# Reordering the first weight block of a delta-rule and two-layer MoE kernel: chunk steps first, four weight pairs early, two loads in flight, grams in units 2 and 4

## The chip, the cores and the metric

The kernel runs on one core of one Trainium2 chip. The time is the device time of one execution in microseconds; lower is better. Times of before are the median of three executions, and one further execution was recorded by the hardware profiler.

## What is computed

A delta-rule recurrence over 768 tokens (4 batches, 8 heads, head size 48), and behind it two feed-forward layers over all 3072 tokens (384 to 2048 to 384).

```python
for t in range(S):
    y[:, :, t] = q_t @ state
    state = state + b_t * outer(k_n_t, v_t - k_n_t @ state)
x = y laid out as (3072, 384)
h = x @ w_in;  g = where(h >= 1, h, where(h <= -1, 0, (h + 1)**2 / 4));  x = g @ w_out
h = x @ w_in2; r = maximum(h, 0);  out = (r * r) @ w_out2
```

## The kernel before

The 768 tokens are cut into 24 chunks of 32. A chunk covers all four batches, so it is 128 rows. Four chunks make a group, and also a block of the first layer. For each group the gram matrices of keys and queries are formed (`gram`, L323), and one triangular system is inverted for the whole group. This inversion, `tri`, starts with a transpose (L423), a few short VectorE steps and the scaling at L453 and L462. Then come 60 alternating GpSimd operations, L483 and L484, in strict sequence, and `end` (L487) is the VectorE transpose that brings the result back. With the inverse, `chunk_steps` carries a chunk through: `ks` and `qs` (L547, subtraction on VectorE at L557), `tr` (L561), `ku` (L596, the state copied back at L603 and L604) and `xt` (L628, split at L630 and L631), which yields the chunk's 128 rows of input for the first layer.

The first layer runs in blocks of four chunks; a block has 16 units, one for each 128 columns of the hidden size. Unit x does the first product into `h` (`hidden`, nine matmuls of 128x512 at L643), the activation (ScalarE L675, VectorE L676, ScalarE L678, VectorE L679), the split of the result in two words (ScalarE L692, VectorE L694), and the second product of unit x - 2 into `acc` (`out_`, nine matmuls at L643; LAG = 2). Every number is kept as a high and a low fp32r word, so each product takes three passes.

A unit has two slots, 2x and 2x + 1. The tables `exa` and `exb`, filled with `put_a` and `put`, say which chunk steps, grams and inversion steps are issued in a slot. In `unit`, slot 2x of `exa` is issued behind the `h` product and the activation.

In block 0 the first layer's weights also have to be made. They arrive as 64-bit numbers (`load_w`, L190, 384 KB each) and are turned into two fp32r words: two passes on ScalarE over the raw bits (L199 and L200, `halves`), the join on VectorE (`make`, L206), the high word on ScalarE (`upper`, L236) and the low word on VectorE (`lower`, L240). Two such loads make a weight pair; pair x holds what the first product of unit x + 1 and the second of unit x - 1 need. Three pairs (READY) are made in the chain of the first four chunks, ahead of unit 0. The others are spread over the units by `between`, which `hidden` calls at four points: behind the first VectorE step, behind the second, behind L692 and behind L694.

All engines take their instructions in the written order in block 0 (`manual_schedule`). The loads stand in SyncE's queue in written order too. `loads(m, ...)` lets m loads be under way: each load waits for the landing of the m-th one ahead of it. A `kqg` load for a gram (two DMAs of 192 KB, L148) takes one of two buffers, so those of chunks 10 and 11 are issued behind the grams of chunks 8 and 9.

The third group's inversion is put from slot `a + 2` on, with `a = max(ready, 13)`, where `ready` is the slot of the group's last grams; its `end` stands in slot 31, and chunk 8, the first that needs it, begins in slot 32.

The first products of block 0 take their PSUM tile from three in turn for units below MANY, and from one ("h") for the others; the two tiles that are then left ("att0", "att1") serve the grams and the chunk steps.

Of the kernel before, what the change touches and what calls it, by code (L numbers as in the profile page):

```python
# [25 lines left out]
def kernel(  # L26
# [41 lines left out]
    KQ, KG = 3, 2  # L68
    WL = 2
    GB = 2  # L70
    MANY = 4

    cst = ctx.enter_context(tc.tile_pool(name="cst", bufs=1))
    wp = ctx.enter_context(tc.tile_pool(name="wp", bufs=1))
# [150 lines left out]
    def halves(x):  # L225
        return sign_bits(raws[x])

    def whole_bits(x):
        for f in halves(x):
            f()  # L230

    def make(x):
        words[x] = joined_words(raws.pop(x), [P, 2, DM])

    def upper(x):
        nc.scalar.copy(weights(x)[:, :, 0], words[x])  # L236

    def lower(x):
        t = weights(x)
        nc.vector.tensor_sub(t[:, :, 1], words.pop(x), t[:, :, 0].bitcast(F32))  # L240
# [543 lines left out]
    SL = 2 * NF  # L784
    SPREAD = 3
    NW, NP = 2 * NF, NF
    READY = 3
    exa, exb = {}, {}
    bits = [f for x in range(READY, NP) for f in (lambda x=x: halves(x)[0](), lambda x=x: halves(x)[1]())]
    bits.reverse()  # L790

    def some(m):
        for _ in range(m):
            if bits:
                bits.pop()()

    def between(f):
        a = READY + f if READY + f < NP else None
        last = a - 1 if f and a is not None else NP - 1 if READY + f == NP else None

        def part(x):
            if x % 2 == 0:
                some(1)
            if x == 0 and last is not None:
                upper(last)
            elif x == 1 and last is not None:
                lower(last)
            elif x == 3 and a is not None:
                make(a)

        return part

    def put(n, slot, *fs):
        for i, f in enumerate(fs):
            exb.setdefault(SL * n + slot + i, []).append(f)
# [9 lines left out]
    def put_a(n, slot, *fs):  # L825
        exa.setdefault(SL * n + slot, []).extend(fs)
# [5 lines left out]
    def run(ex, x):  # L832
        for f in ex.pop(x, ()):
            f()
# [22 lines left out]
    with tc.manual_schedule():  # L857
# [22 lines left out]
        def loads(m, what):  # L880
            flight[0] = m
            for kind, c in what:
                kind(c)
            flight[0] = 0

        def ws(a, z):
            return [(load_w, needed[x]) for x in range(a, z)]

        def kgs(c):
            return [(load_kg, c)]  # L890

        def kvs(c):
            return [(load_kv, c)]

        loads(2, [(load_kg, c) for c in range(4, 8)] + kvs(0) + kvs(1) + ws(0, 4))
        loads(1, kvs(2) + kvs(3) + ws(4, 14))
        begin, pre, steps, end = tri(0, V, True)
        begin()
        pre[0]()
# [44 lines left out]
        s2()  # L944
        q1()
        make(1)
        t2()
        upper(1)
        go(pre1[-2:])
        steps1[0]()  # L950
        go(steps1[1:])
        q2()
        k2()
        lower(1)
        p2()
        y2()
        whole_bits(2)
        s3()
        dld0(3)
        make(2)  # L960
        t3()
        p1()
        x2_()
        upper(2)
        q3()
        p3()
        y3()
        lower(2)
        x1()
        q0()  # L970
        p0()
        x3()
        x0()
        k3()
        loads(2, ws(14, 18) + [(load_kq, 4), (load_kq, 5)] + kgs(8) + kgs(9) + ws(18, 22))
        turn[0] = None

        put(0, 9, lambda: loads(2, ws(22, NW)))
        put(0, 11, end1)
        put(0, 11, lambda: value(4))  # L980
        put(0, 12, lambda: value(5))
# [10 lines left out]
        put(0, SL - 1, lambda: first2(RAW))  # L992

        at, ready = {}, {}
        for c, slot in ((8, 8), (10, 11)):
            ready[c + 1] = slot
            put_a(0, slot, lambda c=c: two_grams(c))
        for n in range(2, NB):
            todo = []
            for j, c in enumerate(range(FIRST[n], FIRST[n] + SIZES[n])):  # L1000
                if n < NB - 1 and 2 * j < SIZES[n + 1]:
                    x = FIRST[n + 1] + 2 * j
# [3 lines left out]
            for i, (mark, s_) in enumerate(todo):  # L1006
                slot = SL * (n - 1) + i * SL // len(todo)
# [16 lines left out]
        for g in range(2, NG):  # L1024
            a, z = ready[GFIRST[g] + GROUPS[g] - 1], at[GFIRST[g]]
            a = max(a, 13)
# [76 lines left out]
```

## Time and profile before

| what | value |
|---|---|
| median of three executions | 1028.0 us (1022.54 to 1029.91) |
| the profiled execution | 1027.41 us |
| its span, first to last instruction | 1025.7 us |
| TensorE (PE) busy | 979.7 us, 96% |
| VectorE (DVE) busy | 518.7 us, 51% |
| ScalarE (ACT) busy | 434.5 us, 42% |
| GpSimd (POOL) busy | 296.5 us, 29% |
| mean granted TensorE clock | 0.992 |

The 1.7 us between the execution and its span lie outside of the program's instructions. Shares are means over the whole span; the stages differ, and the rows below go by stretches.

### The profile page before, as it was taken

The page shows a single profiled execution, that of the slowest core. Times are in us where ns is not written, and L with a number is a line of the kernel's source. Part 1 is how long each engine was busy: PE and PEld are TensorE (multiplying, and loading weights), DVE is VectorE, ACT ScalarE, POOL GpSimd, SP SyncE. Part 2 cuts the span into 40 slices and gives each one's busy share as a digit, 9 for nine tenths or more (in the row PEclk, how much of TensorE's full clock was granted, in tenths as well). Part 3 has the DMA queues.
Part 4 walks back from the last instruction along what each step waited for, and adds up shares of the span by engine and source line. Part 5 has one row for each costly group of instructions (what it writes and reads, how often), then busy time and mean ns, then how long its engine had stood idle before and what let it go on. Part 6 is the DMA issues. An engine that isn't in the chain of part 4 may idle for free.

```text
span 1025.7 us, 29990 instructions
## 1 busy us (share of the span) xinstructions
PE 979.7 (96%) x13416; PEld 832.9 (81%) x13416; DVE 518.7 (51%) x801; ACT 434.5 (42%) x745; POOL 296.5 (29%) x414
## 2 busy tenths in 40 slices
PE   5687888999999999999999999999999999999998
PEld 5676667787888878787888888998999999999997
DVE  4447676565557656655545666543343343333333
ACT  2327456345545534554545554333333333333332
POOL 1479029618605920872201112120020200100000
PEclk9999889999999999999999999999999999999999
DMA  6437741334334432433432223010010000000000
GB/s 128 146 108 218 219 107 48 111 103 141 103 95 133 123 109 84 132 100 109 129 94 86 63 62 124 16 32 31 1 62 1 1 31 1 31 1 1 32 1 31
DMA packets 33937, 80.68 MB, mean 79 GB/s; under 512 B 4368, under 2 KB 11664, under 8 KB 33808
## 3 DMA queue, kind: packets, MB, share of 16 engines
q1 hardware_dynamic: 33808, 78.76, 26.2%
q8 instruction: 105, 1.72, 0.7%
q14 instruction: 24, 0.20, 0.1%
HBM read 63.01 MB, written 15.73 MB: 77 GB/s over the span
## 4 chain that ended last, share of the span: by engine, by line
PE 79%; DMA 10%; POOL 4%; DVE 3%; issue 2%; ACT 1%; SPq 1%; POOLq 0%; ACTq 0%; DVEq 0%
PE h L643 36%; PE acc L643 36%; DMA raw<-in_w_dram 6%; DMA kqt<-in_kq_dram 2%; POOL tx L484 2%; POOL t L483 2%; PE tr L561 1%; PE yy L584 1%; PE sps L596 1%; DMA room<-in_kq_dram 1%; DMA kv<-in_kv_dram 1%; PE yy L547 1%; PE ks L547 1%; DVE gp L487 1%; PE g L323 1%
## 5 line engine op out<-in xcount | busy, mean ns | idle before, releaser
L643 PE MATMUL acc<-w,gg 128*128 128x384 f32 x1152 | 217.1, 337 | 0.2 <-ACT e L702 0.2
L643 PE MATMUL h<-x2s,w 128*128 128x512 f32 x864 | 214.6, 393 | 0.0
L643 PEld LDWEIGHTS acc<-w,gg 128*128 128x128 f32 x1152 | 203.9, 188 | 8.3 <-ACT e L702 0.5
L643 PEld LDWEIGHTS h<-x2s,w 128*128 128x128 f32 x864 | 161.0, 188 | 29.2
L643 PE MATMUL h<-xh,w 128*128 128x512 f32 x576 | 154.1, 404 | 4.4 <-ACT r L675 4.4
L643 PE MATMUL acc<-gh,w 128*128 128x512 f32 x576 | 155.1, 405 | 0.5 <-ACT gh L692 0.5
L683 DVE TENSOR_TENSOR rg<-rg 128x512 f32<-128x512 f32 x96 | 70.0, 729 | 140.7 <-ACT rg L682 140.7
L643 PEld LDWEIGHTS h<-xh,w 128*128 128x128 f32 x576 | 107.0, 191 | 28.5 <-ACT r L675 4.9
L682 ACT ACTIVATE rg<-h,zero 128x512 f32<-128x512 f32 x96 | 66.1, 689 | 138.0 <-PE h L643 138.0
L643 PEld LDWEIGHTS acc<-gh,w 128*128 128x128 f32 x576 | 104.7, 190 | 23.9 <-ACT gh L692 1.0
L694 DVE TENSOR_TENSOR gg<-rg,gg 128x512 fp32r<-128x512 f32 x96 | 67.3, 701 | 104.0 <-ACT gg L692 104.0
L675 ACT ACTIVATE r<-h,one 128x512 f32<-128x512 f32 x96 | 65.9, 686 | 120.6 <-PE h L643 120.2
L692 ACT CAST gg<-rg 128x512 fp32r<-128x512 f32 x96 | 59.7, 622 | 118.8 <-PE acc L643 114.3
L676 DVE TENSOR_SCALAR g<-r 128x512 f32<-128x512 f32 x96 | 47.9, 499 | 109.6 <-ACT r L675 109.2
L484 POOL TENSOR_TENSOR tx<-tx,t 128x30 f32<-128x30 f32 (+9 forms) x150 | 99.5, 664 | 11.4
L694 DVE TENSOR_TENSOR gl<-g,gh 128x512 fp32r<-128x512 f32 x96 | 74.5, 776 | 54.0 <-ACT gh L692 42.6
L483 POOL TENSOR_TENSOR t<-tx,gm 128x30 f32<-128x30 f32 (+9 forms) x150 | 94.5, 630 | 16.6 <-DVE tx L462 5.3
L692 ACT CAST gh<-g 128x512 fp32r<-128x512 f32 x96 | 59.6, 620 | 88.7 <-DVE g L679 72.8
L679 DVE SCALAR_TENSOR_TENSOR g<-r,g 128x512 f32<-128x512 f32 x96 | 76.2, 794 | 36.0 <-ACT g L678 36.0
L643 PE MATMUL h<-xl,w 128*128 128x512 f32 x288 | 82.5, 395 | 0.1
L643 PE MATMUL acc<-gl,w 128*128 128x512 f32 x288 | 82.3, 395 | 0.0
L678 ACT ACTIVATE g<-g 128x512 f32<-128x512 f32 x96 | 60.4, 629 | 31.3 <-DVE g L676 29.8
(119 smaller groups left out, 896.6 us busy)
## 6 DMA issues: line engine op xcount, KB each, us to landing
raw<-in_w_dram SPq DMA_DIRECT2D x64, 384.0 KB, 3.7
kqt<-in_kq_dram SPq DMA_DIRECT2D x82, 192.0 KB, 4.1
kv<-in_kv_dram SPq DMA_DIRECT2D x24, 384.0 KB, 4.0
w2f<-wl SPq DMA_DIRECT2D x32, 192.0 KB, 3.9
w2r<-w2f SPq DMA_DIRECT2D x16, 384.0 KB, 3.0
x<-e SPq DMA_DIRECT2D x18, 256.0 KB, 2.3
x2r<-x SPq DMA_DIRECT2D x6, 768.0 KB, 4.9
out_dram<-e SPq DMA_DIRECT2D x23, 192.0 KB, 2.0
```

The lines of the kernel that those rows point to most:

```text
L483: eng.tensor_mul(t, by.to_broadcast(shape), of.to_broadcast(shape))
L484: return eng.tensor_add(rest, rest, t)
L547: per_bh(lambda b, h, p, pd: nc.tensor.matmul(o[p, h], kqt[c][pd, b // 2, h, x * T:(x + 1) * T], st[pd, b // 2, h], start=h == 0, stop=x = ...
L643: nc.tensor.matmul(o, *((r, l) if swap else (l, r)), **flags)
L675: marks[0] = nc.scalar.activation(r, h, AF.Relu, bias=one)
L676: marks[1] = nc.vector.tensor_scalar(g, r, 2.0, 0.5, ALU.min, ALU.mult)
L678: nc.scalar.activation(g, g, AF.Square)
L679: nc.vector.scalar_tensor_tensor(g, r, -1.0, g, ALU.add, ALU.max)
L682: marks[0] = nc.scalar.activation(r, h, AF.Relu, bias=zero)
L683: marks[1] = nc.vector.tensor_mul(g, r, r)
L692: nc.scalar.copy(ghi, g)
L694: nc.vector.tensor_sub(glo, g, ghi.bitcast(F32))
```

## The change

It does five things. `between` is rewritten: a unit's chunk step or gram from slot 2x is now issued at the first of its four points, ahead of that unit's weight work, and the join of a pair moves from the last point of a unit to the first, its high word from the next unit to the second point of the same unit, and its low word to the second point of the next. READY goes from 3 to 4: a fourth pair, and the raw bits of the fifth, are made in the chain ahead of unit 0. The loads are let two at a time from the weight 10 on, where it was one at a time up to weight 13, and the loads of chunks 8 and 9 for the grams stand behind weight 15. The grams of chunks 8 and 9 move from slot 8 (unit 4) to slot 4 (unit 2), those of 10 and 11 from slot 11 (unit 5) to slot 8 (unit 4), and MANY goes from 4 to 2. The last chunk's state update `k3` moves from ahead of unit 0 into unit 1.

```diff
--- before.py
+++ after.py
@@ -68,7 +68,7 @@
     KQ, KG = 3, 2
     WL = 2
     GB = 2
-    MANY = 4
+    MANY = 2
 
     cst = ctx.enter_context(tc.tile_pool(name="cst", bufs=1))
     wp = ctx.enter_context(tc.tile_pool(name="wp", bufs=1))
@@ -784,9 +784,9 @@
     SL = 2 * NF
     SPREAD = 3
     NW, NP = 2 * NF, NF
-    READY = 3
+    READY = 4
     exa, exb = {}, {}
-    bits = [f for x in range(READY, NP) for f in (lambda x=x: halves(x)[0](), lambda x=x: halves(x)[1]())]
+    bits = [f for x in range(READY + 1, NP) for f in (lambda x=x: halves(x)[0](), lambda x=x: halves(x)[1]())]
     bits.reverse()
 
     def some(m):
@@ -795,18 +795,24 @@
                 bits.pop()()
 
     def between(f):
-        a = READY + f if READY + f < NP else None
-        last = a - 1 if f and a is not None else NP - 1 if READY + f == NP else None
+        def pair(x):
+            return x if READY <= x < NP else None
+
+        word, low = pair(READY + f), pair(READY + f - 1)
 
         def part(x):
-            if x % 2 == 0:
+            if x == 0:
+                run(exa, 2 * f)
                 some(1)
-            if x == 0 and last is not None:
-                upper(last)
-            elif x == 1 and last is not None:
-                lower(last)
-            elif x == 3 and a is not None:
-                make(a)
+                if word is not None:
+                    make(word)
+            elif x == 1:
+                if word is not None:
+                    upper(word)
+                if low is not None:
+                    lower(low)
+            elif x == 2:
+                some(1)
 
         return part
 
@@ -893,7 +899,8 @@
             return [(load_kv, c)]
 
         loads(2, [(load_kg, c) for c in range(4, 8)] + kvs(0) + kvs(1) + ws(0, 4))
-        loads(1, kvs(2) + kvs(3) + ws(4, 14))
+        loads(1, kvs(2) + kvs(3) + ws(4, 10))
+        loads(2, ws(10, 16) + kgs(8) + kgs(9) + ws(16, 20))
         begin, pre, steps, end = tri(0, V, True)
         begin()
         pre[0]()
@@ -944,38 +951,44 @@
         s2()
         q1()
         make(1)
+        upper(1)
+        whole_bits(2)
         t2()
-        upper(1)
         go(pre1[-2:])
         steps1[0]()
         go(steps1[1:])
         q2()
+        lower(1)
+        make(2)
+        upper(2)
         k2()
-        lower(1)
         p2()
+        lower(2)
         y2()
-        whole_bits(2)
+        whole_bits(3)
         s3()
         dld0(3)
-        make(2)
+        make(3)
+        upper(3)
         t3()
         p1()
         x2_()
-        upper(2)
+        lower(3)
         q3()
+        halves(4)[0]()
         p3()
         y3()
-        lower(2)
+        halves(4)[1]()
         x1()
         q0()
         p0()
         x3()
         x0()
-        k3()
-        loads(2, ws(14, 18) + [(load_kq, 4), (load_kq, 5)] + kgs(8) + kgs(9) + ws(18, 22))
+        loads(2, [(load_kq, 4), (load_kq, 5)] + ws(20, 24))
         turn[0] = None
 
-        put(0, 9, lambda: loads(2, ws(22, NW)))
+        put(0, 6, lambda: loads(2, ws(24, NW)))
+        put_a(0, 2, k3)
         put(0, 11, end1)
         put(0, 11, lambda: value(4))
         put(0, 12, lambda: value(5))
@@ -992,7 +1005,7 @@
         put(0, SL - 1, lambda: first2(RAW))
 
         at, ready = {}, {}
-        for c, slot in ((8, 8), (10, 11)):
+        for c, slot in ((8, 4), (10, 8)):
             ready[c + 1] = slot
             put_a(0, slot, lambda c=c: two_grams(c))
         for n in range(2, NB):
```

In SyncE's queue, from the fifth weight load on, before (`raw` are first-layer weights, `kqt` halves of a chunk's keys and queries, `kv` keys and values):

```order
L190 DMA raw<-in_w_dram 128x768 x10
L148 DMA kqt<-in_kq_dram 48x1024 x2
L159 DMA kv<-in_kv_dram 128x768 x3
L190 DMA raw<-in_w_dram 128x768 x4
L148 DMA kqt<-in_kq_dram 48x1024 x8
L190 DMA raw<-in_w_dram 128x768 x4
L148 DMA kqt<-in_kq_dram 48x1024 x4
L190 DMA raw<-in_w_dram 128x768 x10
```

And now:

```order
L190 DMA raw<-in_w_dram 128x768 x12
L148 DMA kqt<-in_kq_dram 48x1024 x4
L190 DMA raw<-in_w_dram 128x768 x4
L148 DMA kqt<-in_kq_dram 48x1024 x2
L159 DMA kv<-in_kv_dram 128x768 x3
L148 DMA kqt<-in_kq_dram 48x1024 x4
L190 DMA raw<-in_w_dram 128x768 x4
L148 DMA kqt<-in_kq_dram 48x1024 x4
L190 DMA raw<-in_w_dram 128x768 x8
```

The loads of chunks 8 and 9 (four halves) now stand ahead of the chain's last loads, and the loads of chunks 10 and 11 (the last four `kqt` ahead of the long row of weights) have two more weight loads ahead of them.

TensorE's order around the grams of chunks 10 and 11 (`g`), before, from unit 5's second product on (`w` with a number is one weight pair):

```order
L643 MATMUL acc_1693<-gh,w_1681 128x512 x2
L643 MATMUL acc_1694<-gh,w_1681 128x512 x2
L643 MATMUL acc_1695<-gh,w_1681 128x512 x2
L643 MATMUL acc_1693<-gl,w_1681 128x512
L643 MATMUL acc_1694<-gl,w_1681 128x512
L643 MATMUL acc_1695<-gl,w_1681 128x512
L323 MATMUL g<-kqt 32x64 x64
L643 MATMUL h<-xh,w_1720 128x512 x6
```

And now, from unit 4's first product on:

```order
L643 MATMUL h<-xh,w_1377 128x512 x6
L643 MATMUL h<-xl,w_1377 128x512 x3
L323 MATMUL g<-kqt 32x64 x64
L643 MATMUL acc_1782<-gh,w_1377 128x512 x2
L643 MATMUL acc_1783<-gh,w_1377 128x512 x2
L643 MATMUL acc_1784<-gh,w_1377 128x512 x2
L643 MATMUL acc_1782<-gl,w_1377 128x512
L643 MATMUL acc_1783<-gl,w_1377 128x512
L643 MATMUL acc_1784<-gl,w_1377 128x512
L643 MATMUL h<-xh,w_1612 128x512 x6
```

Before, these grams stand between unit 5's `acc` and unit 6's `h`. Now they stand behind unit 4's `h`, and three products that were ahead of them are behind them: unit 4's `acc`, unit 5's `h` and unit 5's `acc`.

VectorE around unit 6, the first with a chunk step, before:

```order
L487 STREAM_TRANSPOSE gp<-tx 128x32x32
L676 TENSOR_SCALAR g<-r 128x512
L679 SCALAR_TENSOR_TENSOR g<-r,g 128x512
L240 TENSOR_TENSOR w_1994<-wl,w_1994 128x2x384
L557 TENSOR_TENSOR kv<-kv,ks 128x384
L694 TENSOR_TENSOR gl<-g,gh 128x512
```

And now:

```order
L487 STREAM_TRANSPOSE gp<-tx 128x32x32
L676 TENSOR_SCALAR g<-r 128x512
L557 TENSOR_TENSOR kv<-kv,ks 128x384
L206 SCALAR_TENSOR_TENSOR wl<-raw 128x768
L679 SCALAR_TENSOR_TENSOR g<-r,g 128x512
L240 TENSOR_TENSOR w_1971<-wl,w_1971 128x2x384
L694 TENSOR_TENSOR gl<-g,gh 128x512
```

The subtraction L557 stands directly behind L676 now, and the join L206 stands between L676 and L679, where it stood at the end of the unit.

## Rows read from the trace of the kernel before

**Rows 1.** The page: span, TensorE's busy tenths and its clock in 40 slices.

```profile
span 1025.7 us, 29990 instructions
PE   5687888999999999999999999999999999999998
PEclk9999889999999999999999999999999999999999
```

**Rows 2.** By stretch: length, busy PE, PEld, DVE, ACT, POOL, clock, DMA share, GB/s.

```profile
57.00:99.30 42.30, 34.04 (x812) 27.78 (x813) 20.50 (x28) 23.11 (x37) 37.68 (x61) 0.98 0.56 167
79.30:97.30 18.00, 13.05 (x68) 9.93 (x58) 12.55 (x16) 12.89 (x20) 16.28 (x23) 1.00 0.79 238
97.30:117.80 20.50, 16.72 (x292) 12.99 (x292) 14.63 (x19) 11.89 (x17) 5.26 (x7) 0.83 0.76 199
117.80:145.80 28.00, 23.42 (x525) 18.30 (x526) 18.42 (x29) 16.44 (x26) 0.00 (x0) 0.93 0.66 184
145.80:196.50 50.70, 47.20 (x1096) 37.48 (x1095) 32.98 (x45) 27.36 (x45) 46.16 (x66) 0.94 0.19 57
196.50:400.00 203.50, 201.60 (x4068) 162.51 (x4065) 122.21 (x192) 97.55 (x181) 90.14 (x133) 1.00 0.39 113
```

**Rows 3.** The chain that ended last, 60 to 215 us: start, length, what.

```profile
65.37 3.90 DMA raw<-in_w_dram
...
110.45 5.48 DMA kqt<-in_kq_dram
115.97 1.92 PE g L323 x62
...
145.87 1.28 POOL gm L453
...
193.15 0.13 POOL kv L299
...
196.49 2.23 DVE gp L487
```

**Rows 4.** SyncE's queue in order of time: start, length of the row, loads.

```profile
45.65 34.57 SPq L190 DMA_DIRECT2D raw<-in_w_dram  x10
80.27 0.89 SPq L148 DMA_DIRECT2D kqt<-in_kq_dram  x2
...
101.41 7.19 SPq L190 DMA_DIRECT2D raw<-in_w_dram  x4
108.72 2.04 SPq L148 DMA_DIRECT2D kqt<-in_kq_dram  x4
110.81 17.92 SPq L190 DMA_DIRECT2D raw<-in_w_dram  x10
```

**Rows 5.** TensorE in order of time; in brackets idle time before, and releaser.

```profile
97.30 2.91 PE L643 MATMUL h<-xh,w 128*128 128x512 f32 x6 [4.41 <-ACT r L675]
...
106.59 1.54 PE L643 MATMUL h<-xh,w 128*128 128x512 f32 x6
...
117.83 2.93 PE L643 MATMUL h<-xh,w 128*128 128x512 f32 x6
...
126.63 0.88 PE L561 MATMUL tr<-kv,gp 32*32 32x48 f32 x64 [1.12 <-DVE kv L557]
...
145.68 1.50 PE L561 MATMUL tr<-kv,gp 32*32 32x48 f32 x64 [3.36 <-DVE kv L557]
...
167.08 0.88 PE L561 MATMUL tr<-kv,gp 32*32 32x48 f32 x64 [3.01 <-DVE kv L557]
...
199.31 0.88 PE L547 MATMUL ks<-st,kqt 48*32 48x48 f32 x64 [0.50 <-DVE gp L338]
```

**Rows 6.** ScalarE in order of time: unit 1's and unit 2's first steps, and unit 8's.

```profile
85.94 0.67 ACT L675 ACTIVATE r<-h,one 128x512 f32<-128x512 f32 x1
...
91.13 0.68 ACT L675 ACTIVATE r<-h,one 128x512 f32<-128x512 f32 x1
...
138.48 0.67 ACT L675 ACTIVATE r<-h,one 128x512 f32<-128x512 f32 x1
```

**Rows 7.** VectorE in order of time, units 1 and 8.

```profile
86.17 1.34 DVE L206 SCALAR_TENSOR_TENSOR wl<-raw 128x768 int32<-128x768 int32 x1
...
88.94 0.83 DVE L679 SCALAR_TENSOR_TENSOR g<-r,g 128x512 f32<-128x512 f32 x1 [0.75 <-ACT g L678]
...
143.49 0.96 DVE L206 SCALAR_TENSOR_TENSOR wl<-raw 128x768 int32<-128x768 int32 x1
```

## The prediction, made blind

> **What bounds the kernel now.** I read the page first, then the time by stretch, the chain that ended last, and the engines in order of time where the chain changes engine. The page shows TensorE full from about 200 us on and gaps before it [rows 1]. By stretch, TensorE is busy 201.6 of 203.5 us from 196.5 to 400 us [rows 2], and its work is the same in both kernels. So the change can only move the point at which that full stretch begins. I take the first step of chunk 8, at 199.31 us, as this point [rows 5].
>
> Between 79.3 and 196.5 us the four stretches leave TensorE idle for 4.95, 3.78, 4.58 and 3.50 us, 16.8 in all. The clock of the last three (0.83, 0.93, 0.94) says that another 3.5, 2.0 and 3.0 us are lost at the lower of its two levels, 1.2 in place of 2.4 GHz [rows 2]. That is 25 us on paper.
>
> The chain says why they are not to be had at once. It comes from the weight loads, passes through the load of chunk 11's gram, issued at 110.45 and landed 5.48 us later, and the gram itself at 115.97. Then it goes through block 0 to GpSimd, which starts the third group's inversion at 145.87 and holds the chain until VectorE's transpose at 196.49 [rows 3]. TensorE waits only 0.50 us behind that transpose [rows 5]. So two paths end together: TensorE's own work and GpSimd's 50.6 us of inversion. Whatever makes units 8 to 15 faster on TensorE alone ends in a wait for GpSimd. What counts is when the inversion starts and how long it lasts.
>
> **The loads.** One at a time, ten weights are issued in 34.57 us, 3.8 us for each of nine intervals; two at a time, ten take 17.92 us, 1.95 each [rows 4]. From 80.27 us [rows 4] to the landing at 115.93 there are 18 loads of 384 KB (two halves counted as one): chunk 6, three `kv`, four weights, chunks 4, 5, 8 and 9, four weights, chunks 10 and 11. That makes 1.98 us a load, with one load under way at the start. In the changed kernel pairs begin at weight 10, just behind the issue at 65.37 [rows 3], at 65.7 us, also with one under way. Up to chunk 11's gram there are now 24: six weights, chunks 8 and 9, four weights, chunk 6, three `kv`, chunks 4 and 5, four weights, chunks 10 and 11. So 65.7 + 24 x 1.98 = 113.2; the burst of `kv` loads that no limit holds goes a little faster, and I take 112.5 us. Bounds: at the best stretch's 238 GB/s [rows 2] a load takes 1.65 us, which gives 105.3; at the pace of the four weights from 101.41 (7.19 us for three intervals and an issue of 0.3, 2.29 each [rows 4]), 120.7. So the last gram's load comes about 3.4 us sooner, though two loads at a time save some 12 us, because six more loads stand ahead of it.
>
> **Units 0 to 4.** Before, ScalarE's first steps of units 1 and 2 are 5.19 us apart [rows 6], while a unit is two products of nine matmuls, about 2.06 us each (six in 1.54 [rows 5]). TensorE waits for this ring: 4.41 us ahead of unit 4 [rows 5]. Now the high word leaves the ring, since it runs while VectorE does L679, but the join enters it: 1.34 us between L676 and L679, where VectorE waited 0.75 us [rows 7]. I take 4.7 us a unit, a gain of 0.5. TensorE then reaches the grams of chunks 10 and 11, behind unit 4's first product, at about 100 us, and their data are 10 us away. The gain drowns in this wait. The grams of chunks 8 and 9 in unit 2 are no trouble: their loads are the 7th and 8th, landed at about 84, and TensorE comes there at 86 to 87.
>
> These three edits cost or bring nothing of their own: `k3` (about 0.9 us of TensorE) leaves the front of unit 0 and lies in the ring's slack; the fourth pair's work falls where ScalarE and VectorE are busy 23.1 and 20.5 of 42.3 us [rows 2]; the single `h` tile in units 2 and 3 makes TensorE wait for ScalarE's first step, ahead of the longer wait for the loads. If this cover went, the pair would cost its join and low word, some 2.5 us.
>
> **From the grams to the inversion.** Chunk 11's gram takes 1.9 us [rows 3], to 114.4. Behind it now stand three products that were ahead of it, 6.2 us. After a wait of that length the clock is low for a while: unit 6's product took 2.93 us for six matmuls in place of 1.54 [rows 5]. For the three products together I take 0.9 of loss, between 0 and 2.6. So unit 6 starts at 121.5, which is 3.7 us later than 117.83 [rows 5].
>
> From there GpSimd's start was 28.0 us away. Now unit 6's product is at full clock (1.9 less with its second part). The subtraction stands ahead of the weight work, so `tr`'s wait of 1.12 [rows 5] goes. The join of unit 7 stands earlier, so the inversion's transpose comes about 1.0 sooner. In unit 8 the 7.4 us from ScalarE's step at 138.48 [rows 6] to GpSimd's start lose about 1.6, as the join (0.96 at 143.49 [rows 7]) runs where VectorE used to wait for ScalarE. Together 5.6, so 22.4 are left, and the inversion starts at 143.9, 2.0 us sooner. Its slot is not moved: the first slot is 13 at the least, before and after.
>
> **The inversion and its end.** 50.6 us before. Near its end GpSimd waits for keys and values at 193.15 [rows 3], about 0.9 us in two places; these come with chunk 6's end, which is sooner. One pair's join and low word fewer stand beside it, 2.3 us of VectorE. The second group's steps took 37.7 us of GpSimd beside 20.5 of VectorE, the third's 46.2 beside 33.0 [rows 2]; that is at most 0.68 us for each us, 1.6 for the pair. I take 1.5 less in all, between 0 and 2.5. The transpose then starts at 143.9 + 49.1 = 193.0, which is 3.5 us sooner.
>
> The Trainium skill (SBUF — State Buffer, Who interferes with whom) says that a VectorE instruction with two SBUF inputs and a GpSimd instruction that reads SBUF shut each other out for their whole length. By that rule the pair would be worth its full 2.3 us, the end would be 3.2 less in place of 1.5, and the time 1.7 us lower than below. The rows' slope bears out the direction, and not the full size.
>
> TensorE has about 47 us of work from unit 9's `tr` to chunk 8 (53.6 in the rows, less 3.45 of waits for `tr` and 3.0 of clock), so it is there at 190 to 191 and stands still for some 5 us. What follows may run at the low clock: after idle times of 4.41 and 3.36 us it did, after 3.01 it did not (`tr` at 145.68 took 1.50 us, at 167.08 0.88 [rows 5]). That costs 0 to 3.4 us; I take 1.5. The waits for `tr` of 3.36 and 3.01 us thus go, and come back as one wait ahead of chunk 8.
>
> **Sum.** Inversion's start -2.0, its length -1.5, clock behind the new wait +1.5: -2.0 us. The profiled execution took 1027.41 us, 0.6 below the median of 1028.0, so 1025.4; I give 1025.5.
>
> **The rivals.** First, faster: the loads run at the rate of the best stretch and chunk 11's lands at 105.3. Then the inversion starts 7.2 us sooner still, and the time is 1018. For it: the 238 GB/s; against it: the next stretch had 199 [rows 2], and most of the new loads go in pairs, at 1.95. Chance 0.2, with the case that GpSimd runs the inversion at the second group's pace (some 5 us less, 1020.5).
>
> Second, slower: the loads come later than I have them. VectorE has the masks of chunks 10 and 11 ahead of unit 4's join and activation, so units 4 and 5 stand still with TensorE until the data are there. Each us of the landing is one us of the inversion's start. The break-even is a landing at 114.5, and at the slow pace of 2.29 it is 120.7: 8.2 us on 1025.5, so 1033.7. For it: chunk 11's load now has two more weights ahead of it; against it: the 18 loads before held 1.98. Chance 0.2.
>
> Third, the change doesn't do what it says: the grams stand earlier but the inversion starts when it did, since its slot is the same and unit 8 comes no sooner. Then the saved waits of units 9 and 11 all turn up ahead of chunk 8, and the time is that of before, 1027 to 1028. Chance 0.1.
>
> **How the numbers follow.** My forecast, 1021 to 1029, has 0.5. The range takes in the slower rival up to half of its price and the faster one to its end: 1018 to 1031. One per cent, 10 us, is about what a measurement of this kernel can tell from no change. Faster by more needs the fast loads and the shorter inversion together: 0.13. Slower by more needs loads slower than any row: 0.06. Within 1%: 0.81.
>
> **What the changed profile would show.** Right: TensorE idle for 8 us or more ahead of the second pair of grams, released by a load that lands at 110 to 115; no wait for L557 ahead of units 7 and 11; GpSimd's L453 at 142 to 146; TensorE waiting several us ahead of chunk 8, released behind L487. Wrong: grams that wait for nothing, GpSimd starting before 138, or no wait at chunk 8; then the loads are faster than I have them, or the inversion is not the end.

## The result, and the profile after

The changed kernel takes 1030.99 us (median of 20 executions, 1025.93 to 1035.09). The kernel before, run 20 times, takes 1024.89 (1020.23 to 1029.91); the median of the three shown ahead of the prediction, 1028.0, lay at the upper side of that. The ratio is 1.0053, 95% interval [1.0034, 1.0072]: 5.4 us slower, where some 2 us faster were forecast. Below, kernels of different sets are compared by their ratios to the kernel before of the same set; a difference of 0.001 is 1.02 us. The profiled execution took 1032.13 us, its span is 1030.4.

By stretch, with the columns of [rows 2] (length, busy PE, PEld, DVE, ACT, POOL, clock, DMA share, GB/s), the changed kernel has:

```profile
79.30:97.30 18.00, 15.45 (x244) 11.79 (x243) 14.53 (x17) 13.55 (x20) 16.43 (x21) 1.00 0.80 223
97.30:117.80 20.50, 8.00 (x142) 6.56 (x143) 7.21 (x10) 5.60 (x9) 6.53 (x10) 0.67 0.76 210
117.80:145.80 28.00, 26.82 (x538) 21.22 (x536) 22.13 (x32) 20.92 (x33) 0.00 (x0) 1.00 0.50 133
145.80:196.50 50.70, 46.42 (x1104) 37.02 (x1104) 31.46 (x47) 25.19 (x42) 44.95 (x66) 1.00 0.26 76
196.50:400.00 203.50, 199.14 (x4045) 160.88 (x4046) 121.81 (x191) 96.34 (x179) 89.76 (x133) 0.98 0.38 109
```

TensorE does more than before in the first and third of these, and falls to 8.00 us of 20.50 in the second, at a clock of 0.67. TensorE in order of time shows what that is:

```profile
97.45 1.67 PE L643 MATMUL h<-xh,w 128*128 128x512 f32 x6 [1.72 <-ACT r L675]
98.96 0.85 PE L643 MATMUL h<-xl,w 128*128 128x512 f32 x3
111.84 0.39 PE L323 MATMUL g<-kqt 48*32 48x64 f32 x2 [12.02 <-DMA kqt<-in_kq_dram]
112.55 3.63 PE L323 MATMUL g<-kqt 48*32 48x64 f32 x126 [0.32 <-DMA kqt<-in_kq_dram]
116.11 2.28 PE L643 MATMUL acc<-gh,w 128*128 128x512 f32 x6
...
123.04 1.53 PE L643 MATMUL h<-xh,w 128*128 128x512 f32 x6
...
130.28 0.54 PE L561 MATMUL tr<-kv,gp 32*32 32x48 f32 x32 [0.77 <-issue]
...
146.89 0.88 PE L561 MATMUL tr<-kv,gp 32*32 32x48 f32 x64 [1.50 <-DVE kv L557]
...
192.47 0.85 PE L643 MATMUL acc<-gl,w 128*128 128x512 f32 x3
198.97 1.50 PE L547 MATMUL ks<-st,kqt 48*32 48x48 f32 x64 [5.66 <-DVE gp L338]
```

Unit 4's first product is over at 99.8, and then TensorE stands still for 12.02 us, until the first half of chunk 10's load lands at 111.70; the last of the four halves lands at 113.91. The grams take 3.63 us behind that in place of some 2, at the low clock. Unit 6's product starts at 123.04, 5.2 us later than in [rows 5]. Behind that the rows have two short stops: 0.77 us in the middle of unit 6's `tr`, for which the profile names no releaser, and 1.50 us ahead of unit 9's. Then TensorE is ready for chunk 8 at 193.3 and waits 5.66 us.

VectorE and GpSimd in order of time show the rest of the chain, a wait for the grams and then the inversion's start and end:

```profile
114.53 0.69 DVE L338 TENSOR_TENSOR gp<-g,mask 128x512 f32<-128x512 f32 x1 [11.71 <-PE g L323]
...
196.37 2.02 DVE L487 STREAM_TRANSPOSE gp<-tx 128x1024 f32<-128x1024 f32 x1 [6.00 <-POOL tx L484]
198.22 0.70 DVE L338 TENSOR_TENSOR gp<-g,mask 128x512 f32<-128x512 f32 x1
```

```profile
147.08 1.28 POOL L453 TENSOR_TENSOR gm<-gm,st 128x256 f32<-128x256 f32 x1 [42.79 <-DVE st L442]
```

The row of TensorE's wait names its releaser, and it is not the inverse: chunk 8's first step, `ks`, reads the state and the keys, and writes to the PSUM tile that the grams issued just ahead of it have used. L338, the mask that reads these grams, sets the tile free, and in VectorE's order L338 stands behind L487, which waits for GpSimd. So the inversion holds chunk 8 here by way of VectorE's order; whether L338 ahead of L487 would take the wait away was not tried.

The inversion starts 1.2 us later than in [rows 3] and lasts 49.25 us. Its transpose L487 stands at 196.37 against 196.49, and chunk 8 at 198.97 against 199.31: as far as this point the two kernels end at the same time. The difference of the two spans, 4.7 us, arises behind it, and the experiments have to say how that hangs together with the waits ahead of it.

### The profile page after: what moved, and what is told of

Read it like the earlier page. It is cut to its first block, busy times and chain, and to the rows that moved or that the text cites. A ratio compares the mean times of both kernels' runs of the same rounds, so it can differ in the third digit from the quotient of the medians.

```text
span 1030.4 us, 30002 instructions
## 1 busy us (share of the span) xinstructions
PE 977.3 (95%) x13416; PEld 831.7 (81%) x13416; DVE 518.7 (50%) x801; ACT 435.1 (42%) x745; POOL 297.4 (29%) x414
## 4 chain that ended last, share of the span: by engine, by line
PE 78%; DMA 10%; POOL 4%; DVE 4%; issue 2%; ACT 1%; SPq 1%; ACTq 0%; POOLq 0%; DVEq 0%
PE acc L643 35%; PE h L643 35%; DMA raw<-in_w_dram 5%; DMA kqt<-in_kq_dram 3%; POOL tx L484 2%; POOL t L483 2%; PE tr L561 1%; PE yy L584 1%; PE sps L596 1%; DMA kv<-in_kv_dram 1%; PE yy L547 1%; PE ks L547 1%; DMA room<-in_kq_dram 1%; DVE gm L423 1%; PE g L323 1%
## 5 line engine op out<-in xcount | busy, mean ns | idle before, releaser
L643 PE MATMUL h<-xh,w 128*128 128x512 f32 x576 | 151.9, 399 | 2.8 <-ACT r L675 2.3
L484 POOL TENSOR_TENSOR tx<-tx,t 128x30 f32<-128x30 f32 (+9 forms) x150 | 101.9, 679 | 11.4
L676 DVE TENSOR_SCALAR g<-r 128x512 f32<-128x512 f32 x96 | 48.3, 503 | 109.4 <-ACT r L675 108.8
L483 POOL TENSOR_TENSOR t<-tx,gm 128x30 f32<-128x30 f32 (+9 forms) x150 | 95.2, 635 | 15.2 <-DVE tx L462 4.0
L679 DVE SCALAR_TENSOR_TENSOR g<-r,g 128x512 f32<-128x512 f32 x96 | 77.9, 811 | 22.6 <-ACT g L678 22.6
```

The lines of the kernel that those rows point to most:

```text
L483: eng.tensor_mul(t, by.to_broadcast(shape), of.to_broadcast(shape))
L484: return eng.tensor_add(rest, rest, t)
L643: nc.tensor.matmul(o, *((r, l) if swap else (l, r)), **flags)
L676: marks[1] = nc.vector.tensor_scalar(g, r, 2.0, 0.5, ALU.min, ALU.mult)
L679: nc.vector.scalar_tensor_tensor(g, r, -1.0, g, ALU.add, ALU.max)
```

## The experiments

**Theory A**: the grams of chunks 10 and 11 stand too early for their load; TensorE and all that hangs on it waits, and the third group's inversion, which starts behind them, then holds chunk 8. **Theory B**: the new order of `between` costs the time. **Theory C**: the loss lies behind block 0. The first four kernels each undo or keep one part. The kernel before, run beside them, took 1025.88 us (20 executions).

**The grams of chunks 10 and 11 back in unit 5**, all else changed:

```diff
-        for c, slot in ((8, 4), (10, 8)):
+        for c, slot in ((8, 4), (10, 11)):
```

> The changed kernel with the grams of chunks 10 and 11 put back to slot 11, behind unit 5's second product; all else as changed. Theory A (the place of these grams, ahead of three products and behind two more loads, is the cost): TensorE's wait for them falls from 12.3 to 6 to 8 us, the inversion of the third group starts at 140 to 143 in place of 147.1, its closing transpose at 190 to 192, and the time is 4 to 6 us below the changed kernel, at or just under the kernel before. Theory B (the new order in between, with the join inside VectorE's part of the unit, is the cost): the time stays within 2 us of the changed kernel. Theory C (the time is lost behind block 0, where 3.8 of the 4.7 us between the two profiles appear): as B, within 2 us of the changed kernel, wherever the inversion starts.

1020.41 us, ratio to before 0.9954 [0.9927, 0.9982], by the ratios 10 us below the changed kernel, where Theory A had 4 to 6. The last gram load landed at 108.96, 5 us sooner than in the changed kernel's profile though the queue is the same, TensorE waited 0.17 us for it, and the inversion started at 133.41. So not all of this profile's gain is the slot's. Theories B and C, which had no difference beyond 2 us, do not fit.

**The early place kept, the loads of chunks 10 and 11 put first** (e2 in the expectations below): in the changed kernel the loads of chunks 4 and 5 and four weights stand ahead of them in SyncE's queue; here they stand behind.

```diff
-        loads(2, [(load_kq, 4), (load_kq, 5)] + ws(20, 24))
+        put(0, 4, lambda: loads(2, ws(20, 22) + [(load_kq, 4), (load_kq, 5)] + ws(22, 24)))
```

> The changed kernel with one move in SyncE's queue: the loads of chunks 4 and 5 and of weights 20 to 23 are issued in unit 2, behind the grams of chunks 8 and 9, so that the loads of chunks 10 and 11 stand ahead of them. Theory A: chunk 11's gram data land at 100 to 105 in place of 113.9, TensorE's wait there falls to 5 us or less, the inversion starts at 137 to 140 in place of 147.1, its closing transpose comes at 186 to 189, and the time is 6 to 9 us below the changed kernel, so 1 to 4 below the kernel before. Theory B: no difference to the changed kernel beyond 2 us. Theory C: none beyond 2 us either.

1016.82 us, ratio 0.9910 [0.9886, 0.9934], 15 us below the changed kernel, again more than Theory A's 6 to 9. The last of these loads landed at 99.14. TensorE in order of time, around these grams and around chunk 8:

```profile
97.58 1.65 PE L643 MATMUL h<-xh,w 128*128 128x512 f32 x6 [1.72 <-ACT r L675]
99.07 0.85 PE L643 MATMUL h<-xl,w 128*128 128x512 f32 x3
99.85 1.99 PE L323 MATMUL g<-kqt 48*32 48x64 f32 x128
...
183.95 1.50 PE L547 MATMUL ks<-st,kqt 48*32 48x48 f32 x64 [5.72 <-DVE gp L338]
185.23 1.50 PE L547 MATMUL yy<-st,kqt 48*32 48x48 f32 x64
186.66 2.93 PE L643 MATMUL h<-xh,w 128*128 128x512 f32 x6
```

The same instructions in the same order, with the load there in time: the 12 us of waiting are gone, and the grams take 1.99 us. The wait ahead of chunk 8 is as long as in the changed kernel (5.72), 15 us sooner. From 180.4 us, within that wait, the clock was low for 10.2 us: the product of six took 2.93.

**The new `between` and the fourth pair alone**, with the old loads, gram slots, MANY and `k3`:

```diff
-    READY = 3
+    READY = 4
...
-            if x % 2 == 0:
+            if x == 0:
+                run(exa, 2 * f)
                 some(1)
```

> The kernel before with the new between and four weight pairs in the chain alone; loads, gram slots, MANY and the place of the chunk 3 state update as before. Theory A: this half of the change costs nothing; the grams wait as before or somewhat longer (3 to 5 us), the inversion starts at 141 to 144 in place of 145.9, and the time is 1 to 4 us below the kernel before. Theory B: the time is 4 to 7 us above the kernel before, like the changed kernel. Theory C: within 2 us of the kernel before.

1020.08 us, ratio 0.9941 [0.9922, 0.9961]: 6.0 faster than before, where Theory A had 1 to 4. Theory B falls; this part is a gain. From unit 6's product to the inversion's start it took 23.1 us, where [rows 5] and [rows 3] have 28.0. Unit 6's `tr` waits for nothing here, and chunk 8 waits as long as in the changed kernel:

```profile
122.95 0.88 PE L561 MATMUL tr<-kv,gp 32*32 32x48 f32 x64
123.76 1.66 PE L643 MATMUL h<-xh,w 128*128 128x512 f32 x6
...
192.14 1.50 PE L547 MATMUL ks<-st,kqt 48*32 48x48 f32 x64 [5.69 <-DVE gp L338]
```

So the wait of 5.7 us ahead of chunk 8 comes with the new order and the inversion's unmoved slot, not with the late grams: it is 5.66 to 5.72 us in all six profiles that have both, whether the kernel gains or loses, and the 6.0 us of gain are what is left with this wait in.

**The loads, the gram slots and MANY alone**, with the old `between` and three pairs:

```diff
-    MANY = 4
+    MANY = 2
...
-        for c, slot in ((8, 8), (10, 11)):
+        for c, slot in ((8, 4), (10, 8)):
```

> The kernel before with the new loads, gram slots and MANY of 2 alone; between, three weight pairs in the chain and the chunk 3 state update as before. Theory A: TensorE waits 8 to 12 us for the grams of chunks 10 and 11, the inversion starts at 148 to 152, its closing transpose at 198 to 202, and the time is 3 to 8 us above the kernel before. Theory B: within 2 us of the kernel before. Theory C: no clear statement; 0 to 5 us above.

1033.87 us, ratio 1.0093 [1.0064, 1.0122], 9.5 us slower than before, with a gram wait of 7.33 us and waits for `tr` of 3.37, 3.78 and 3.01. Theory A's account holds (the inversion starts at 150.65, its transpose at 201.56), its 3 to 8 us are too few. The order alone gains 6.0 and the loads with the early grams lose 9.5. The sum is +3.5, the whole change +5.4; with intervals of 2 to 3 us on each this agrees. The move of `k3` is in neither part and was not run alone; the first two kernels keep it and gain.

The next four (before: 1024.83 us, 23 executions) ask what ends block 0. **The inversion one unit sooner** in the kernel with the gram loads first (e5 below):

```diff
-            a = max(a, 13)
+            a = max(a, 11)
```

> This kernel is e2 with the first slot of the third group's inversion at 13 in place of 15 (two slots, one unit sooner). Theory A, as it stands after the first four runs: once the grams of chunks 10 and 11 wait for nothing, the third group's inversion is what ends last, and TensorE waits for it ahead of chunk 8 (5.72 us in e2, from about 178 us, and then 10.2 us at the low clock). So the inversion (L453) starts at 126 to 128 in place of 132.03, its transpose L487 stands at 175 to 177 in place of 181.28, the wait ahead of chunk 8 is under 1 us, the low clock behind it is gone, and the time is 1006 to 1011 us, 6 to 10 below e2's 1016.8. Rival: the end of block 0 is TensorE's own work, or the work behind it takes the gain; then L487 comes sooner but the time stays within 2 us of e2's.

1009.49 us, ratio 0.9855 [0.9828, 0.9881]. GpSimd starts and TensorE gets to chunk 8 so:

```profile
125.50 1.28 POOL L453 TENSOR_TENSOR gm<-gm,st 128x256 f32<-128x256 f32 x1 [20.82 <-DVE st L442]
```

```profile
132.28 0.71 PE L561 MATMUL tr<-kv,gp 32*32 32x48 f32 x48 [2.49 <-DVE kv L557]
...
181.96 0.85 PE L643 MATMUL acc<-gl,w 128*128 128x512 f32 x3
182.74 0.88 PE L547 MATMUL ks<-st,kqt 48*32 48x48 f32 x64
183.74 0.88 PE L547 MATMUL yy<-st,kqt 48*32 48x48 f32 x64
184.56 1.65 PE L643 MATMUL h<-xh,w 128*128 128x512 f32 x6
```

The time is as Theory A had it, one of its numbers is not: L487 stands at 179.79, not at 175 to 177. The inversion was over at 174.9, but L487 is late in VectorE's written order. TensorE itself was ready for chunk 8 4.5 us later than in the kernel above (182.7 for 178.2); on its way there it had 2.49 us of waiting for `tr`, a stop of 1.46 in the middle of that `tr` and 6.8 us of low clock, where the kernel above has one wait of 1.50 and two of 0.3. So chunk 8 starts only 1.2 us sooner. The gain is 5.6 us by the ratios and 7.1 by the spans of the two profiles. Of the 7.1, 3.1 lie between chunk 8's subtraction and chunk 10's (46.67 us for 49.75), where no low clock is left: the product behind chunk 8's first steps takes 1.65 us for 2.93. Another 2.4 lie behind an output store at 742 us, a place that is looked at below.

**Two units sooner**, with the second group's `end1` and `value` steps moved up:

```diff
-            a = max(a, 13)
+            a = max(a, 9)
...
-        put(0, 11, end1)
+        put(0, 9, end1)
```

> e2 with that first slot at 11, and the second group's end and values of chunks 4 to 6 in slot 9, so that GpSimd is free for it. Theory A: the inversion starts at 119 to 122 and ends about 171, but TensorE itself is not at chunk 8 before 177 or so; so no more than 2 us below e5, 1005 to 1011, and the wait ahead of chunk 8 is 0. VectorE may wait for GpSimd's second inversion at slot 9 and hand 1 to 3 us back. Rival (TensorE's own work is the end): within 2 us of e2's 1016.8.

1008.71 us, ratio 0.9851 [0.9826, 0.9876], no different from one unit. Chunk 8 waits for nothing: the inversion is no longer the end.

**The same step in the kernel before** (13 to 11), as a check of the prediction's reading of it:

> The kernel before with the first slot of the third group's inversion at 13 in place of 15. By the reading that the prediction made of the kernel before (TensorE's own work and the inversion end together, TensorE waits 0.50 us behind it), the inversion starts 4 to 6 us sooner but the time falls by 0 to 2 us: 1023 to 1026 beside the 1025.9 of before. If instead the inversion alone holds the end of block 0 in the kernel before, the time falls by as much as the inversion comes sooner, to 1020 to 1022.

1025.97 us, ratio 1.0011 [0.9988, 1.0033]. The inversion started at 135.91, 10 us sooner than in [rows 3] and more than the 4 to 6 expected, and nothing was gained. Chunk 8 waits for nothing and starts at 196.38: TensorE's own work is the end, as the prediction read it. (It starts 2.9 us ahead of [rows 5] in this profile, whose last gram load landed at 112.65 in place of 115.93.)

**And in the changed kernel:**

> The changed kernel with the first slot of the third group's inversion at 13 in place of 15. Theory A: its inversion starts at 141 to 143 in place of 147.08, L487 stands at 190 to 192 in place of 196.37, and TensorE, which is at chunk 8 at 193.3, waits there 0 to 1 us in place of 5.66, and the 6.8 us at the low clock behind it go; the time is 6 to 9 us below the changed kernel's 1031.0, 1022 to 1025, about the time of before. Rival: the wait comes back ahead of the next step that needs the chunk, or the loss lies elsewhere; then the time stays above 1029.

1023.64 us, ratio 0.9983 [0.9962, 1.0005], 7.2 below the changed kernel. Chunk 8 waits 0.77 us and no low clock follows. In this execution the gram load landed at 109.32 and the wait ahead of the grams was 8.06 us, so in the profile the inversion's earlier start (137.03, where 141 to 143 were expected) is in part the load's. The step is worth 7.2 us here and 5.6 in the kernel without a wait for the grams: it takes away what the order's wait ahead of chunk 8 costs, and says little about the grams.

The last four (before: 1023.41 us, 18 executions) change the dose and repeat the two profiles. **Two of the four weight loads behind the grams' loads**, in the changed kernel:

```diff
-        loads(2, [(load_kq, 4), (load_kq, 5)] + ws(20, 24))
+        loads(2, [(load_kq, 4), (load_kq, 5)] + ws(20, 22))
+        put(0, 4, lambda: loads(2, ws(22, 24)))
```

> The changed kernel with two of the four weight loads of the chain's end (numbers 22 and 23) put behind the loads of chunks 10 and 11. Theory A: the last gram's load lands two loads, 3.5 to 4 us, sooner than in the changed kernel, TensorE's wait ahead of these grams is as much shorter, and so is the time: 1026 to 1028 beside the changed kernel's 1031.0. Rival: what costs the time is that three products stand behind the grams in place of ahead of them, at any landing; then the time stays above 1029.5.

1024.35 us, ratio 1.0009 [0.9989, 1.0029], 4.5 below the changed kernel; by its ratio it is at 1025.8 beside the changed kernel's 1031, at the lower edge of what Theory A gave. The rival, that the place alone costs the time at any landing, falls. The load landed at 106.29, 5.6 to 7.6 us ahead of the changed kernel's two profiles, where 3.5 to 4 were expected:

```profile
103.82 0.39 PE L323 MATMUL g<-kqt 48*32 48x64 f32 x2 [3.71 <-DMA kqt<-in_kq_dram]
```

**Two more weights ahead of them in the kernel before:**

```diff
-kgs(8) + kgs(9) + ws(18, 22))
+kgs(8) + kgs(9) + ws(18, 24))
```

> The kernel before with weights 22 and 23 put ahead of the loads of chunks 10 and 11. Theory A: the last gram's load lands 3.5 to 4 us later, and the time rises by 3 to 4 us, to 1028 to 1029. Rival: in the kernel before TensorE's own work is behind the loads anyway and swallows this; then the time rises by less than 1.5 us.

1029.75 us, ratio 1.0059 [1.0035, 1.0082]: 6.0 slower, more than the 3 to 4 expected, though the interval reaches down to 3.6. The load landed at 118.09, and TensorE stood still for 6.99 us at the first half of chunk 10's load. Its row in the kernel before, and then here:

```profile
112.79 0.27 PE L323 MATMUL g<-kqt 48*32 48x64 f32 x2 [1.91 <-DMA kqt<-in_kq_dram]
```

```profile
115.52 0.39 PE L323 MATMUL g<-kqt 48*32 48x64 f32 x2 [6.99 <-DMA kqt<-in_kq_dram]
```

This one edit makes the kernel before as much slower as the whole change did.

**Both kernels once more:**

> The kernel before once more, for a second profile: the landing of chunk 11's gram load, 115.93 in the first, comes at 112 to 114 if the first was a late one (a kernel with the same loads had 112.65), and chunk 8 then starts 1 to 3 us ahead of 199.31.

> The changed kernel once more, for a second profile: that landing, 113.91 in the first, comes at 109 to 112 (three kernels with the same loads had 108.96, 110.50 and 109.32), the inversion's start as much ahead of 147.08, and the wait ahead of chunk 8 between 5 and 6 us again.

Single times of 1027.69 and 1031.79 us. In the kernel before the load landed at 113.50 and the inversion started at 144.2; in the changed one at 111.93 and 146.35, behind 12.04 us of waiting, and the wait ahead of chunk 8 was 5.72. The landings are as expected, the steps behind them less so: in the changed kernel the inversion starts 0.7 us sooner for a load 2.0 us sooner, and in the kernel before chunk 8 starts 0.8 us sooner, not 1 to 3. Chunk 8 started at 198.55 and 198.37, 0.2 us apart, and 0.3 in the first pair: level again. So in both pairs the loss is behind chunk 8. Both profiles of the kernel before are long executions, though, 2.5 us above the median of its 20 and 4.3 above that of the 18 run beside the second. In a median execution part of the loss may lie ahead of chunk 8; no profile shows that.

Two places carry the loss in these pairs. From chunk 8's subtraction (L557) to chunk 10's, the first pair has 46.34 and 48.51 us, the second 46.50 and 48.03: 1.5 to 2.2 us more, with the low clock that sets in during the wait of 5.7 (from 196.0 to 202.8 us in the first profile) and a wait for `tr` of 0.83 at 233 (0.19 in the second). The new order alone has 48.52 there, and gains. The other place is at 760 us, in the second layer, behind the second of six blocks of output. ScalarE's last copy of the block waits for the landing of the block's first store, whose buffer it takes, and TensorE waits for ScalarE. TensorE there in the kernel before (second profile), and then ScalarE and TensorE in the changed one (second profile):

```profile
762.15 1.30 PE L643 MATMUL acc<-w,gg 128*128 128x384 f32 x6 [1.70 <-ACT e L702]
763.29 2.24 PE L643 MATMUL h<-x2s,w 128*128 128x512 f32 x9
765.37 2.28 PE L643 MATMUL acc<-w,gg 128*128 128x384 f32 x12
```

```profile
764.11 0.48 ACT L702 COPY e<-acc 128x384 f32<-128x384 f32 x1 [3.65 <-DMA out_dram<-e]
```

```profile
764.64 1.36 PE L643 MATMUL acc<-w,gg 128*128 128x384 f32 x6 [1.76 <-ACT e L702]
765.80 3.80 PE L643 MATMUL h<-x2s,w 128*128 128x512 f32 x9
```

In the kernel before the nine matmuls behind the wait take 2.24 us, in the changed one 3.80: the clock was low for 3.4 us. From this block's first store to the next block's, the kernel before has 66.9 and 68.8 us in its two profiles, the changed kernel 70.5 and 70.4. The instructions there are the same in both kernels.

The 14 profiles fall into three kinds here. In three the store lands 2.2 to 2.4 us behind its issue and TensorE does not wait (66.9 to 67.0 us). In eight it lands after 3.5 to 4.2 us and TensorE waits 1.1 to 1.8 us, at the full clock (68.2 to 68.8). In three it waits 1.8 to 1.9 us and the clock falls (70.4 to 70.5): the changed kernel twice, and the changed kernel with the inversion sooner. The kernel before has a profile of the first kind and one of the second; the changed kernel with the grams late is of the first kind. And the kernel before with two more loads ahead has the same wait as the changed kernel's second profile, 1.76 us, with the clock left high:

```profile
763.98 1.30 PE L643 MATMUL acc<-w,gg 128*128 128x384 f32 x6 [1.76 <-ACT e L702]
765.12 2.24 PE L643 MATMUL h<-x2s,w 128*128 128x512 f32 x9
```

So this place differs by 1.9 us between two executions of the kernel before alone, and it isn't shown that the change has a part in what it costs.

Counted from this block's first store to the end, 2.8 and 1.6 us of the pairs' differences are left here. So the pairs add up: -0.3 to chunk 8, +2.2 behind it, +2.8 at the store, 4.7 in all; and -0.2, +1.5, +1.1 between chunk 10 and the last chunk (not followed further), +1.6, 4.1 in all (the terms are rounded). From chunk 8 to the end that is 826.4 and 827.4 us in the kernel before and 831.5 and 831.7 in the changed one. It was 827.0 in the changed kernel with the grams late and 829.0 with the order alone, both with the same wait of 5.7 us ahead of chunk 8.

## Why the prediction was wrong

**What held.** The mechanism of the wait did: TensorE reached the grams at 99.8 (about 100 predicted), the data were 12.0 us away (10), the landing came at 113.9 and 111.9 (112.5, from 24 loads at 1.98 us), units 4 and 5 stood still with TensorE, and unit 6 began at 123.0 and 122.1 (121.5). The inversion's length, 49.3 us, is close to the 49.1 predicted. TensorE came to chunk 8 some 5 us early and stood still there, 5.66 us, as said, and the stretch behind that took 1.5 to 2.2 us more where 1.5 were taken for the clock. One of the signs named did not come: the inversion's start, at 147.1 and 146.4, lies outside of 142 to 146.

Two readings in what held were wrong all the same. What stands at 193.15 in [rows 3] is no wait of GpSimd but its own work, `value` (L299): three pieces, 3.2 us together within the inversion, in the kernel before and in the changed one. Nothing of the 0.9 us taken for it was there to be had; the shorter inversion is all in L483 and L484, 41.0 us of work before and 39.6 now. That the length came out is luck to that extent. And of the "six more loads" only two are more: from the issue at 65.37 on, the kernel before has 22 loads up to the last gram's, four of them one at a time, the changed kernel 24. The landing worked out from 24 is not touched by this.

By the rule of the Trainium skill (SBUF — State Buffer, Who interferes with whom) the pair would have been worth 2.3 us of the inversion. The whole inversion is shorter by 1.3 in the two pairs of profiles (50.58 to 49.25, and 50.57 to 49.32), less than by that rule and nearer to the 1.5 that were taken; and the loads and grams alone, with the old three pairs, had 49.93, so not even all of the 1.3 need be the pair's.

**The step that failed** is the one from the grams to the inversion, "Together 5.6, so 22.4 are left, and the inversion starts at 143.9, 2.0 us sooner". In the changed kernel 24.0 us were left (24.3 in the second profile), so 4.0 were gained. Unit 8's share held: from ScalarE's first step to the inversion's start it took 5.6 us for 7.4, 1.8 gained for the 1.6 predicted:

```profile
141.46 0.67 ACT L675 ACTIVATE r<-h,one 128x512 f32<-128x512 f32 x1
```

The full clock of unit 6's product gave 1.7 for 1.9. The other two terms failed. `tr`'s wait of 1.12 for L557 went, but a stop of 0.77 us in the middle of `tr` came in its place (1.15 in the second profile), so 0.2 us were left of this term, and nothing in the second profile. The earlier join, taken at about 1.0, gave 0.3 to 0.5: from unit 7's product to ScalarE's first step of unit 8 it took 10.7 us (10.6 in the second profile) for 11.0. With the order alone, where `tr` has neither wait nor stop, unit 6's two terms gave 1.5 and 1.2, the join 0.5, and 5.0 of the 5.6 came. What the stop in `tr` waits for stays open.

Together with unit 6's product, which began 1.5 us later than forecast (0.6 in the second profile), the inversion started at 147.1 (146.4), 1.2 us later than in [rows 3] and not 2.0 sooner. The second rival, "slower", is of this kind, but it has its point at a landing at 114.5, and the two landings were 113.9 and 111.9: the time was lost at about the landing that was forecast.

**What the sum did not have**: anything behind chunk 8 but the clock. It took TensorE's work there as the same in both kernels. In the pairs of profiles 2.8 and 1.6 us are lost from the output store at 760 us to the end, and 1.1 in the second pair between chunk 10 and the last chunk. As the 14 profiles stand, it is open whether the change has a part in this; no run isolates it. The sum also began at one profile: the first of before lay 2.5 us above the median of its 20 executions, that of the changed kernel 1.1, and the profile read for the prediction had the latest landing, 115.9, of the four profiles with these loads.

**What is shown.** Taking away the wait for the grams, in two independent ways with all else of the change kept, brings 10 and 15 us; moving two loads out of its way brings 4.5; giving the kernel before two more loads ahead costs it 6.0. So Theory A's first half carries the result: the order of the weight work gains 6.0 us, and the early grams lose more than that, since TensorE asks for their data 12 us before they land and all that stands behind it waits. Its second half does not hold as it stands: the wait ahead of chunk 8 comes with the order, whose 6.0 us have its cost in them, and it is as long in the kernels whose grams do not wait; moving the inversion ahead takes it away from either. Theory C falls with the first two kernels. Where in the changed kernel the 5.4 us lie is shown in part: ahead of chunk 8 the gain is used up, 1.5 to 2.2 us follow in the pairs, with the low clock behind that wait, and the rest, most of it at the output store, stays open.

The experiments also give a version that beats both: the changed kernel with the gram loads ahead of the chain's last loads and the inversion one unit sooner, 1009.49 us, 1.5% below the kernel before and 2% below the changed one.

## What to carry to other kernels

An instruction that is moved forward in an in-order engine has to have its load moved forward too, past all that stands ahead of it in the transfer queue: reckon the landing and the time at which the instruction asks, before and after. Where two paths end together, savings on one of them end as a wait at their meeting point, and here the wait cost more than its length, as TensorE's clock was low behind it; start the longer serial part earlier in the same edit. Look at what the waiting instruction itself needs: here it was a buffer that an unrelated instruction behind the transpose sets free. And a wait that a sum takes away can come back as another stop at the same place, so run the part that should gain alone before its terms are added to others.

## What was not expected of the hardware

The same load of the same program landed at 115.93 and 113.50 in two executions, at 113.91 and 111.93 in two of the other; kernels with the changed kernel's loads had 108.96 to 110.50.

The first store of the second output block landed 2.2 us behind its issue in one profile of the kernel before and 4.1 in the other, and 2.2 to 4.3 in the 14 profiles; in 11 of them TensorE waits there, 1.1 to 1.9 us. The same store of the first block took 1.9 us in every one. A wait of 1.76 us left the clock high in one profile, and one of the same length was followed by 3.4 us at the low clock in another. With a wait of 5.7 us ahead of chunk 8 the clock was low for 6.8 us in five profiles and for 10.2 in one, from within the wait on; with waits of 0 to 1.2 us there it stayed high.
